# A fused attention and FFN kernel: v loaded by head over 128 partitions, and the order of loads and casts that goes with it

## The chip, the cores and the metric

The kernel runs on one core of one Trainium2 chip. The metric is the time of one execution in device microseconds. A core has five engines with an instruction queue each: TensorE (PE, its weight loads PEld), VectorE (DVE), ScalarE (ACT), GpSimd (POOL) and SyncE (SP), which here only issues DMAs. The DMAs themselves run on 16 DMA engines.

## The reference

Attention with a polynomial sketch as its feature map, over 4 batches, 4 heads, 1088 tokens and heads of 32, followed by a gated FFN on the 4352 tokens of width 128:

```
def phi(x):                                   # 64 features of a token
    a = einsum('rd,bhsd->bhsr', S1, x)        # r = 8
    b = einsum('rd,bhsd->bhsr', S2, x)
    return einsum('bhsi,bhsj->bhsij', a, b).reshape(..., 64)
q_p, k_p = phi(q), phi(k)
kv  = einsum('bhsf,bhsd->bhfd', k_p, v)
z   = sum(k_p, axis=2)
out = einsum('bhsf,bhfd->bhsd', q_p, kv) / (einsum('bhsf,bhf->bhs', q_p, z) + 1e-6)

x = out, tokens by 128 (4 heads x 32)
y = (maximum(x @ w_gate, 0) * (x @ w_val)) @ w_out      # d_ff = 1536, float32 in and out
```

## The kernel before

**Layout of the tokens.** A batch's 1088 tokens of a head lie over 32 partitions, 34 (NC) consecutive tokens each. For k and q the four heads are stacked, so partition 32 h + p holds tokens 34 p to 34 p + 33 of head h, and one load fills 128 partitions with rows of 4352 bytes. v is wanted the other way round: partition 32 a + p holds, for each of the four heads, tokens 34 p + 9 a to 34 p + 9 a + 8 (KX = 9 columns of 32 numbers, 1152 bytes). The tile `v32[b]` is therefore [128, 4 heads, 288]. The fourth block (a = 3) runs two tokens over the end of its row, and the last two columns of those partitions are left out later by `KV_ROWS`; for the very last row of v the two tokens don't exist, so that load is shorter and line 309 clears the place.

`load_v(eng, b, a)` (L212 to L218) loads one block a: 32 partitions, 4 heads, 288 numbers. Four of them load a batch, in the order 0, 2, 1, 3.

**Stages.** For each batch: class `K` takes k: DVE transposes in blocks of 32 (`t1`, L525), TensorE applies the sketch (`sk`, L536), DVE transposes back (`t2`, L549), `z` and `w` make the denominator's vector (L564, L578), POOL or DVE builds the 64 features (`phi`, L593), ACT casts v to float16 (`vc`, L599, two heads at a time), and TensorE sums features times v (`kv`, L606), which DVE writes into a block-diagonal tile `bz` (L613). Class `Q` does the same for q (L728, L734, then the denominator on POOL and DVE), and class `G` builds the q features for a group of up to 512 tokens (L859, POOL), has them transposed, multiplies them by `bz` (`num`, L893), and ACT writes the result to `xT` (L905), the input of the FFN. The transposes of the first three groups are done by TensorE (L877, copied out by ACT, L884), those of the other seven by a transposing DMA that SP issues (`xpose`, L867).

Class `F` is one FFN unit, 512 columns: `g` (L950, TensorE) and `relu` (L955, ACT), `v` (L962, TensorE), the product on DVE (L972) or, for every sixth unit, on POOL after a copy by ACT (L967, L977), and `o` (L984), which adds up w_out's part. There are 103 units. Units 0 to 23 belong to batch 0, 24 to 95 to batches 1 to 3, and the last 7 to the tokens left over from all batches. After a group's last unit ACT copies the sum (L992) and SP stores it with four DMAs of 32 partitions (L1001), the last group with one (L1006).

**The order of the work.** Nothing is ordered by hand on the five engines. Class `Plan` holds every operation with its engine, an assumed duration, its predecessors, its PSUM banks and a due time, runs through them in a simulated order of time, and the instructions are then issued in that order; each engine works its own list strictly in order. The assumed times are the small functions `dve`, `act`, `pool`, `pe16`, the constants T0, U and D1 (first unit, distance of units, a later shift), and the table LAND of landing times of the first loads. In the planned gaps of TensorE before the first unit, `warm` (L326 to L331) puts dummy matmuls.

The first loads are issued by SP in the order of the text: k of batch 0 in two parts, q of batch 0 in two parts, v of batch 0, w_gate and w_val thirds 0 and 1, w_out third 0, k of batch 1, the last thirds, and q of batch 1. The weights are float32 in DRAM; they are loaded into tiles of later batches (`wst`: k_sb and q_sb of batch 3, k_sb of batch 2, v32 of batches 1 and 2) and cast from there (`CAST`). A later load into such a tile waits for the cast. The later loads (`load`) are planned on SP with the stores and the transposing DMAs.

**DMAs and semaphores.** In the built program SP's transfers go round eight semaphores. Each transfer waits until the one that used its semaphore before, the eighth back, has landed.

Of the kernel before, what the change touches and what calls it, by code (L numbers as in the profile page):

```python
# [146 lines left out]
def kernel(  # L147
# [12 lines left out]
    nc = tc.nc  # L160

    B, H, S, D = q.shape
# [48 lines left out]

    def load_v(eng, b, a):  # L212
        w = KX * D
        n = w if a < 3 or b < B - 1 else (KX - 2) * D
        src = v[b, 0]
        eng.dma_start(
            out=v32[b][32 * a:32 * a + 32, :, 0:n],
            in_=bass.AP(src.tensor, src.offset + a * w, [[NC * D, 32], [S * D, H], [1, n]]))  # L218

# [55 lines left out]
    def load_vs(b):  # L275
        for a in (0, 2, 1, 3):
            load_v(nc.sync, b, a)

# [104 lines left out]
    l_sx = Lease()  # L383
    T0, U, SLACK = 11.0, 0.68, 0.25
    D1 = 0.2

# [11 lines left out]
    def act(cols):  # L398
        return cols / 1200.0 + 0.045

    def pool(cols):
        return cols * 0.00188 + 0.07

    LAND = {"k0a": 3.6, "S": 4.3, "k0b": 4.25, "q0a": 5.6, "q0b": 7.35, "v0": 9.95,
            "wg0": 10.35, "wv0": 11.0, "wg1": 11.65, "wv1": 12.3, "wo0": 12.95, "k1": 15.6,
            "wg2": 16.25, "wv2": 16.9, "wo1": 17.5, "wo2": 18.1, "q1": 19.5}
    land = {n: P.landed(n, t) for n, t in LAND.items()}
    P.free["DMA"] = LAND["q1"]

    def bank(l, i=0):  # L410
# [22 lines left out]


    def load(name, fn, after):
# [7 lines left out]
    load("v2", lambda: load_vs(2), [wcast["wg2"], wcast["wv2"], land["v1"]])  # L443
    load("k3", lambda: load_k(nc.sync, 3), [wcast["wg0"], wcast["wv0"], land["q2"]])
    load("q3", lambda: load_q(nc.sync, 3), [wcast["wg1"], wcast["wv1"], land["q2"]])
    load("v3", lambda: load_vs(3), [land["v2"]])

    class K:


        def __init__(self, b, prev):
# [179 lines left out]
    class Q:  # L631
# [3 lines left out]
        def __init__(self, b, x0, n, i, ks, qt1, old):  # L635
# [9 lines left out]
            if first:  # L645
                la, lc = Lease(), Lease()
                self.la, self.lc = la, lc
                s1 = [P.add("PE", f"qsk {name} {x}", 0.48, lambda x=x: self.sk_tok(x, x + 2),
                            qt1 + [wb_op], take=[la]) for x in range(0, n, 2)]
                t2 = P.add("ACT", f"qt2 {name}", act(2 * cols), self.t2_tok, s1 + old, drop=[la],  # L650
                           rec=0.13)
                la.left += n
                lt = Lease()
                self.lt = lt
                at = P.add("PE", f"qaT {name}", 0.85, self.aT, qt1 + [sa_op], take=[lt])
                ate = P.add("ACT", f"qaTe {name}", act(256), self.aTe, [at], drop=[lt], rec=0.13)
                s2 = [P.add("PE", f"qc {name}", 0.45, self.cx, [ate, ks[0].zc_op], take=[lc])]
                o1 = P.add("DVE", f"bw {name}", dve(cols) + 0.03, self.mul_ps, s2 + [t2] + old,
                           drop=[lc], rec=0.09)
                e, eng = "DVE", nc.vector  # L660

            else:
                self.l4 = [Lease(2), Lease(2)]
                s1 = P.add("PE", f"qsk {name}", cols / 600.0 + 0.28 + 0.37 * (n > NX),
                           self.sk, qt1 + wcs + [wq_op], take=self.l4)
# [133 lines left out]
    class G:  # L799


        def __init__(self, qs, b, ks, x0, n, i, col, old, how):
# [12 lines left out]
            else:  # L815
                phis.append(P.add("POOL", f"qphi {name}", pool(n * 256),
                                  lambda: self.phi(nc.gpsimd, 0, n), [qs.o4] + old))
            if how == "DMA":
                pt = P.add("SP", f"qtd {name}", 1.28, self.xpose, phis + old, rec=0.7)
                pt = P.add("DMA", f"qtd {name}", 0.6, None, [pt], rec=0.5)  # L820
            else:
# [85 lines left out]
    class F:  # L907


        def __init__(self, u, grp, qg, js, prev, old):  # L910
# [13 lines left out]
                      due=t + 0.35)  # L924
            vv = P.add("PE", f"v {u}", cost, self.v, [qg.x_op, wcast[f"wv{third}"]], take=[lv], due=t + 0.2)
            if self.pool:
                a2 = P.add("ACT", f"vcp {u}", act(cols), self.vcp, [vv], drop=[lv], rec=0.13,
                           due=t + 0.6)
                h = P.add("POOL", f"hp {u}", 1.18, self.hp, [a, a2, old], due=t + 1.3)
            else:  # L930
# [112 lines left out]
    for n, (b, x0, w, parts) in enumerate(sets):  # L1043
# [6 lines left out]
        for gb, y, m in parts:  # L1050
# [43 lines left out]
    for o in todo:  # L1094
        if o.eng == "PE":
            if not kept and o.start < f0 + 0.1:
                warm(int((o.start - at) * (1200 if o.start < WARM else 2280)))
# [33 lines left out]
```

## Time and profile before

| | |
|---|---|
| median of 3 runs (lowest, highest) | 102.06 us (101.67, 102.32) |
| profiled execution: time, span | 102.56 us, 100.8 us |
| granted TensorE clock | 1.00 throughout |
| busy: PE, PEld, DVE, ACT, POOL | 95.1, 66.4, 83.8, 82.2, 59.9 us |
| DMA | 13.28 MB, 16783 packets |
| HBM read, written | 9.14 MB, 2.23 MB |
| first FFN matmul (L950) | 13.76 us |
| v of batch 0: first issue, first cast | 2.63 us, 9.99 us |
| dummies (L330) | 85 matmuls, 7.7 us |

Times inside a profile count from the start of the span. Busy time of an engine is the time in which at least one of its instructions runs; PE's instructions overlap, so a busy PE is not PE at its peak. "Idle before" a group is idle time of its engine, put down to what ended it. A DMA's time to landing counts from its issue, so it holds its wait behind earlier transfers. SPq is SP's sequencer: what it shows is the time to issue a DMA, not the transfer.

### The profile page before, as it was taken

What the parts mean: (1) busy time and instruction counts of PE and PEld (TensorE: products, weight loads), DVE (VectorE), ACT (ScalarE), POOL (GpSimd) and SP (SyncE); (2) the same over time, 40 slices, a digit from 0 to 9 for tenths busy, and PEclk for the clock granted to TensorE, in tenths of its full rate; (3) what the DMA queues carried; (4) which work ended last, traced back from release to release, by engine and by line L of the source; (5) the groups of instructions that cost most, each with busy time, mean ns of one, the idle gap of its engine ahead of it and who ended that gap; (6) DMA issues with size and microseconds to landing.
All of it is one profiled execution on the core that took longest, in us unless ns stands there. A gap on an engine that the chain in (4) does not pass through costs nothing.

```text
span 100.8 us, 3139 instructions
## 1 busy us (share of the span) xinstructions
PE 95.1 (94%) x1191; PEld 66.4 (66%) x1191; DVE 83.8 (83%) x181; ACT 82.2 (82%) x162; POOL 59.9 (59%) x64
## 2 busy tenths in 40 slices
PE   6999997999999899999999999999999999999960
PEld 6959895678775466656756676667666666667940
DVE  5989959899999989999998679978768587795960
ACT  3411968997999978999977769899899999989940
POOL 7157269399999399349973993489960314033100
PEclk9999999999999999999999999999999999999999
DMA  2999999499943696300426003001481300120031
GB/s 44 321 272 294 408 403 417 166 309 272 386 131 108 145 136 163 104 7 0 104 52 156 7 0 104 7 7 37 121 182 37 81 24 0 52 59 0 4 100 52
DMA packets 16783, 13.28 MB, mean 132 GB/s; under 512 B 8064, under 2 KB 14464, under 8 KB 16768
## 3 DMA queue, kind: packets, MB, share of 16 engines
q1 hardware_dynamic: 16736, 13.08, 45.8%
q8 instruction: 9, 0.15, 0.6%
q14 instruction: 6, 0.05, 0.1%
q10 hardware_dynamic: 32, 0.00, 0.0%
HBM read 9.14 MB, written 2.23 MB: 113 GB/s over the span
## 4 chain that ended last, share of the span: by engine, by line
PE 78%; POOL 7%; ACT 5%; DMA 3%; issue 2%; DVE 2%; ACTq 0%
PE ps L984 19%; PE ps L950 18%; PE ps L962 17%; PE ps L330 7%; POOL qqp L859 4%; PE ps L893 3%; ACT g_sb L955 3%; PE ps L728 3%; DMA qpt<-qqp 3%; PE ps L536 2%; PE ps L606 2%; POOL kp L593 1%; PE ps L564 1%; PE ps L877 1%; DVE qabc L734 1%
## 5 line engine op out<-in xcount | busy, mean ns | idle before, releaser
L972 DVE TENSOR_TENSOR ht<-g_sb,ps 128x512 f16<-128x512 f16 (+1 forms) x87 | 55.4, 672 | 10.1 <-ACT g_sb L955 5.5
L955 ACT ACTIVATE g_sb<-ps 128x512 f16<-128x512 f32 (+1 forms) x103 | 57.1, 610 | 4.9 <-PE ps L950 4.1
L950 PE MATMUL ps<-xT,wg 128*128 128x512 f16 (+1 forms) x120 | 38.3, 348 | 0.4 <-ACT wg L425 0.4
L984 PEld LDWEIGHTS <-ht 128*128 128x128 f16 x408 | 28.8, 98 | 14.0 <-POOL ht L977 2.5
L984 PE MATMUL ps<-wo,ht 128*128 128x128 f16 x408 | 36.5, 219 | 0.2
L962 PE MATMUL ps<-xT,wv 128*128 128x512 f16 (+1 forms) x120 | 36.5, 348 | 0.0
L977 POOL TENSOR_TENSOR ht<-g_sb,v_sb 128x512 f16<-128x512 f16 x16 | 18.7, 1170 | 19.3 <-ACT v_sb L967 13.2
L593 POOL TENSOR_TENSOR kp<-kab 128x512 f16<-128x512 f32 (+1 forms) x15 | 17.1, 1162 | 5.0 <-DVE kab L549 5.0
L962 PEld LDWEIGHTS <-wv 128*128 128x128 f16 x120 | 13.0, 115 | 5.1 <-issue 1.1
L859 POOL TENSOR_TENSOR qqp<-qan,qabc 128x1024 f16<-128x1024 f32 (+1 forms) x9 | 15.7, 1763 | 0.1
L950 PEld LDWEIGHTS <-wg 128*128 128x128 f16 x120 | 13.1, 114 | 3.7 <-issue 0.9
L967 ACT COPY v_sb<-ps 128x512 f32<-128x512 f32 x16 | 9.7, 605 | 0.0
L330 PE MATMUL ps<-zero 128*128 128x128 f16 (+2 forms) x85 | 7.7, 257 | 1.0 <-DVE maskkv L295 1.0
L330 PEld LDWEIGHTS <-zero 128*128 128x128 f16 x85 | 6.7, 119 | 1.4 <-DVE maskkv L295 1.0
L992 ACT ACTIVATE o_sb<-ps 128x512 f32<-128x512 f32 (+1 forms) x10 | 5.5, 546 | 1.9 <-PE ps L984 1.9
L599 ACT CAST v<-v 128x576 f16<-128x576 f32 x8 | 5.3, 700 | 1.5 <-DMA v<-in_v_dram 1.4
L734 DVE STREAM_TRANSPOSE qabc<-ps 128x512 f32<-128x512 f32 (+2 forms) x8 | 5.4, 695 | 0.7 <-PE ps L728 0.6
L1024 DVE STREAM_TRANSPOSE qT<-q_sb 128x576 f32<-128x576 f32 (+4 forms) x10 | 6.0, 611 | 0.0
L905 ACT CAST xT<-ps 128x512 f16<-128x512 f32 (+1 forms) x9 | 4.9, 550 | 1.1 <-PE ps L893 1.1
L893 PE MATMUL ps<-qpt,bz 128*128 128x512 f16 (+2 forms) x26 | 5.3, 305 | 0.4 <-DMA qpt<-qqp 0.4
L525 DVE STREAM_TRANSPOSE kT<-k_sb 128x544 f32<-128x544 f32 (+2 forms) x8 | 5.6, 725 | 0.0
L606 PEld LDWEIGHTS <-kp 128*128 128x128 f16 (+1 forms) x72 | 3.6, 98 | 1.3 <-issue 0.2
(85 smaller groups left out, 63.9 us busy)
## 6 DMA issues: line engine op xcount, KB each, us to landing
v<-in_v_dram SPq DMA_DIRECT2D x15, 144.0 KB, 4.5
out_dram<-o_sb SPq DMA_DIRECT2D x28, 64.0 KB, 1.7
k_sb<-in_k_dram SPq DMA_DIRECT2D x3, 544.0 KB, 5.4
q_sb<-in_q_dram SPq DMA_DIRECT2D x3, 544.0 KB, 7.1
k_sb<-in_moe_w_out_dram SPq DMA_DIRECT2D x2, 256.0 KB, 5.9
q_sb<-in_q_dram SPq DMA_DIRECT2D x1, 416.0 KB, 5.2
k_sb<-in_k_dram SPq DMA_DIRECT2D x1, 288.0 KB, 2.9
k_sb<-in_k_dram SPq DMA_DIRECT2D x1, 256.0 KB, 3.0
```

The costliest lines, as they stand in the source:

```text
L330: nc.tensor.matmul(PS[:, W_BANK, 0:m], zero, zero[:, 0:m], start=True, stop=True)
L593: eng.tensor_tensor(out=self.kp[:, lo:hi].rearrange("p x g (i a c) -> p (x g i) a c", i=2, a=R), in0=src[:, 0, :, :, None].to_broadcast([1 ...
L734: nc.vector.transpose(self.abc[:, 0:self.n, 2 * i:2 * i + 2].rearrange("p x h f -> p h x f"), PS[:, b0:b1 + 1, 0:self.n * 32].rearrange("p ...
L859: eng.tensor_tensor(out=self.qp[:, lo:hi].rearrange("p x g (i a c) -> p (x g i) a c", i=2, a=R), in0=a_in[:, :, :, None].to_broadcast([128 ...
L893: nc.tensor.matmul(o[:, 0:n * 128].rearrange("f (x t) -> f x t", x=n)[:, :, t], self.ks[b or 0].bz[:, p], self.pt[:, 0:n, p, t], start=(p ...
L950: nc.tensor.matmul(bank(self.lg)[:, y * W:(y + 1) * W], wblock(wg, j), x, start=True, stop=True, skip_group_check=True)
L955: nc.scalar.activation(out=self.gs[:, 0:self.cols], in_=bank(self.lg)[:, 0:self.cols], func=ACTF.Relu)
L962: nc.tensor.matmul(bank(self.lv)[:, y * W:(y + 1) * W], wblock(wv, j), x, start=True, stop=True, skip_group_check=True)
L967: nc.scalar.copy(out=self.vs, in_=bank(self.lv))
L972: nc.vector.tensor_tensor(out=self.ht[:, 0:w], in0=self.gs[:, 0:w], in1=bank(self.lv)[:, 0:w], op=ALU.mult)
L977: nc.gpsimd.tensor_tensor(out=self.ht, in0=self.gs, in1=self.vs, op=ALU.mult)
L984: nc.tensor.matmul(o[:, s], self.ht[:, y * W + s * 128:y * W + (s + 1) * 128], wo[:, j // 4, (j % 4) * DM:(j % 4 + 1) * DM], start=(j == 0 ...
```

## The change

- `load_v` takes a head instead of a block: one DMA for all 128 partitions of one head, 1152 bytes each, into the same tile in the same layout. The DRAM side of it is written as 4 blocks (step 288) by 32 rows (step 1088) by 288 numbers. The last head of the last batch is split into 96 and 32 partitions, so there are 17 v loads instead of 16.
- The plan lets the cast of the first pair of heads of batch 0 depend on the first two loads alone (`v0a`, `v0b`).
- The weights' last thirds of w_gate and w_val and the second third of w_out are issued ahead of k of batch 1.
- `warm` makes dummies of up to 512 columns, by reading the zero tile repeatedly, and leaves 0.1 us of each later gap free.
- The casts of wv0 and wv1 move from POOL to ACT, that of wv2 from ACT to POOL; of the two blocks of batch 0's k features that DVE made, one goes to POOL.
- The loads of k, q and v of batch 3 are planned after the transposing DMA of the group `gs[4]` (the second of batch 1).
- Assumed times in the plan: the table LAND, U, D1, `act`, a v load's issue (0.62 instead of 0.44 each) and transfer, and some others.

```
-    def load_v(eng, b, a):
+    def load_v(eng, b, h):
         w = KX * D
-        n = w if a < 3 or b < B - 1 else (KX - 2) * D
-        src = v[b, 0]
-        eng.dma_start(
-            out=v32[b][32 * a:32 * a + 32, :, 0:n],
-            in_=bass.AP(src.tensor, src.offset + a * w, [[NC * D, 32], [S * D, H], [1, n]]))
+        src = v[b, h]
+
+        for lo, hi, n in [(0, 4, w)] if (b, h) != (B - 1, H - 1) else [(0, 3, w), (3, 4, w - 2 * D)]:
+            eng.dma_start(
+                out=v32[b][32 * lo:32 * hi, h, 0:n],
+                in_=bass.AP(src.tensor, src.offset + lo * w, [[w, hi - lo], [NC * D, 32], [1, n]]))
...
-    for a in (0, 2, 1, 3):
-        load_v(nc.sync, 0, a)
+    for h in range(H):
+        load_v(nc.sync, 0, h)
...
     load_w(0)
     load_w(1)
     load_wo(0)
-    load_k(nc.sync, 1)
     load_w(2)
     load_wo(1)
+    load_k(nc.sync, 1)
     load_wo(2)
...
     def load_vs(b):
-        for a in (0, 2, 1, 3):
-            load_v(nc.sync, b, a)
+        for h in range(H):
+            load_v(nc.sync, b, h)
...
-    nc.vector.memset(v32[B - 1][96:128, :, (KX - 2) * D:], 0.0)
+    nc.vector.memset(v32[B - 1][96:128, H - 1, (KX - 2) * D:], 0.0)
...
         while n >= 32:
-            m = min(n // 32 * 32, 128)
-            nc.tensor.matmul(PS[:, W_BANK, 0:m], zero, zero[:, 0:m], start=True, stop=True)
-            n -= m
+            m, w = (min(n // 128, 4), 128) if n >= 128 else (1, n // 32 * 32)
+            nc.tensor.matmul(PS[:, W_BANK, 0:m * w], zero,
+                             zero[:, None, 0:w].to_broadcast([128, m, w]), start=True, stop=True)
+            n -= m * w
...
-    T0, U, SLACK = 11.0, 0.68, 0.25
-    D1 = 0.2
+    T0, U, SLACK = 11.0, 0.69, 0.25
+    D1 = 0.7
...
-    CAST = {"wg0": "ACT", "wv0": "POOL", "wg1": "ACT", "wv1": "POOL", "wo0": "POOL",
-            "wg2": "ACT", "wv2": "ACT", "wo1": "ACT", "wo2": "POOL"}
+    CAST = {"wg0": "ACT", "wv0": "ACT", "wg1": "ACT", "wv1": "ACT", "wo0": "POOL",
+            "wg2": "ACT", "wv2": "POOL", "wo1": "ACT", "wo2": "POOL"}
...
-        i = P.add("SP", f"{name} issue", 0.44 * n, fn, after, rec=1.95 - 0.44 * n)
-        land[name] = P.add("DMA", name, 2.7 if n == 4 else 1.4, None, [i], rec=0.15)
+        issue[name] = i = P.add("SP", f"{name} issue", (0.62 if n == 4 else 0.44) * n, fn, after,
+                                rec=(1.95 - 0.62 * n if n == 4 else 1.5))
+        land[name] = P.add("DMA", name, 1.5 if n == 4 else 1.4, None, [i], rec=0.15)
...
-            own = [3, 4] if b == 0 else []
+            own = [4] if b == 0 else []
...
-            vc = [P.add("ACT", f"vc {b} {h}", 0.58, lambda h=h: self.vc(h), [land[f"v{b}"]],
-                        rec=0.13) for h in range(2)]
+            vc = [P.add("ACT", f"vc {b} {h}", 0.58, lambda h=h: self.vc(h),
+                        [land[f"v{b}" if b else f"v0{'ab'[h]}"]], rec=0.13) for h in range(2)]
...
+    for n in ("k3", "q3", "v3"):
+        issue[n].after.append(gs[4].turn)
+        gs[4].turn.succ.append(issue[n])
```

SP's order after the first loads, in the built programs: before, q of batch 2, k2, v1, k3, q3, four stores, v2, four stores, two transposing DMAs, v3; after, q2, k2, v1, v2, eight stores, two transposing DMAs, k3, q3, v3.

More of the change, by code (lines that the diff above doesn't have):

```diff
@@ L398, in act @@
     def act(cols):
-        return cols / 1200.0 + 0.045
+        return cols / 1200.0 + 0.062
     def pool(cols):
         return cols * 0.00188 + 0.07
-    LAND = {"k0a": 3.6, "S": 4.3, "k0b": 4.25, "q0a": 5.6, "q0b": 7.35, "v0": 9.95,
-            "wg0": 10.35, "wv0": 11.0, "wg1": 11.65, "wv1": 12.3, "wo0": 12.95, "k1": 15.6,
-            "wg2": 16.25, "wv2": 16.9, "wo1": 17.5, "wo2": 18.1, "q1": 19.5}
+    LAND = {"k0a": 3.6, "S": 4.3, "k0b": 4.25, "q0a": 5.2, "q0b": 6.9, "v0a": 7.7, "v0b": 8.45,
+            "wg0": 9.3, "wv0": 9.94, "wg1": 10.58, "wv1": 11.22, "wo0": 11.86, "wg2": 12.5,
+            "wv2": 13.14, "wo1": 13.78, "k1": 16.14, "wo2": 16.78, "q1": 18.14}
     land = {n: P.landed(n, t) for n, t in LAND.items()}
@@ L443 @@
     load("v2", lambda: load_vs(2), [wcast["wg2"], wcast["wv2"], land["v1"]])
-    load("k3", lambda: load_k(nc.sync, 3), [wcast["wg0"], wcast["wv0"], land["q2"]])
-    load("q3", lambda: load_q(nc.sync, 3), [wcast["wg1"], wcast["wv1"], land["q2"]])
+    load("k3", lambda: load_k(nc.sync, 3), [wcast["wg0"], wcast["wv0"]])
+    load("q3", lambda: load_q(nc.sync, 3), [wcast["wg1"], wcast["wv1"]])
     load("v3", lambda: load_vs(3), [land["v2"]])
@@ L815, in __init__ @@
             else:
-                phis.append(P.add("POOL", f"qphi {name}", pool(n * 256),
+                phis.append(P.add("POOL", f"qphi {name}", pool(n * 256) - 0.02 * n,
                                   lambda: self.phi(nc.gpsimd, 0, n), [qs.o4] + old))
@@ L819, in __init__ @@
                 pt = P.add("SP", f"qtd {name}", 1.28, self.xpose, phis + old, rec=0.7)
+                self.turn = pt
                 pt = P.add("DMA", f"qtd {name}", 0.6, None, [pt], rec=0.5)
@@ L924, in __init__ @@
                       due=t + 0.35)
-            vv = P.add("PE", f"v {u}", cost, self.v, [qg.x_op, wcast[f"wv{third}"]], take=[lv], due=t + 0.2)
+            vv = P.add("PE", f"v {u}", cost, self.v, [qg.x_op, wcast[f"wv{third}"]], take=[lv], rec=0.07,
+                       due=t + 0.2)
             if self.pool:
@@ L928, in __init__ @@
                            due=t + 0.6)
-                h = P.add("POOL", f"hp {u}", 1.18, self.hp, [a, a2, old], due=t + 1.3)
+                h = P.add("POOL", f"hp {u}", 1.13, self.hp, [a, a2, old], rec=0.06,
+                          due=t + 1.3)
             else:
```

6 lines of the change are left out of this document (4 added, 2 removed).

## The prediction

> **What bounds the kernel now.** I read the page first, then the chain of waits in order of time, the DMA views, and SP's and ACT's timelines around the place where the chain leaves TensorE.
>
> ```profile
> span 100.8 us, 3139 instructions
> PE 95.1 (94%) x1191; PEld 66.4 (66%) x1191; DVE 83.8 (83%) x181; ACT 82.2 (82%) x162; POOL 59.9 (59%) x64
> ```
>
> TensorE is busy almost throughout, so anything that only shifts work elsewhere is worth nothing unless it moves the times at which TensorE gets its inputs. The chain shows where those decide:
>
> ```profile
> 26.50 0.59 POOL qan L794
> 27.09 0.06 POOL ht L977
> 27.15 1.02 issue
> 28.17 3.88 POOL qqp L859 x2
> 32.05 0.28 POOL ht L977
> 32.33 2.79 DMA qpt<-qqp
> 35.12 0.04 issue
> 35.17 0.60 PE ps L893 x2
> ```
>
> Line 893 at 35.17 makes the features of batch 1, the first of the last 79 FFN units. From there the chain is TensorE almost without a break to 97.4, so the time is "arrival of batch 1" plus a tail of about 62 us. A later arrival moves the end one for one once units 0 to 23 have run out. Here TensorE had run out only just:
>
> ```profile
> 14.00:18.00 4.00, 3.07 (x32) 2.40 (x29) 3.18 (x6) 3.39 (x7) 3.79 (x5) 1.00 1.04 408
> ...
> 32.00:35.20 3.20, 2.80 (x36) 1.35 (x34) 3.20 (x6) 3.20 (x8) 1.52 (x3) 1.00 0.54 124
> ```
>
> (The first figure after the length is TensorE's busy time, the last two are DMA share and GB/s.) It idled 0.9 us in one stretch and 0.4 us in the other; so little slack can hide nothing large.
>
> The arrival hangs on SP's queue. Its first transposing DMA is issued at 32.33, though the first qqp was done at about 30.1 (half of 3.88 after 28.17):
>
> ```profile
> 25.61 4.66 SPq L216 DMA_DIRECT2D v<-in_v_dram  x4
> 30.37 1.79 SPq L1001 DMA_DIRECT2D out_dram<-o_sb  x4
> 32.33 2.68 SPq L867 DMA_TRANSPOSE qpt<-qqp  x2
> ```
>
> SP hands its transfers to eight semaphores in turn, and each waits for the one eight back to land. So batch 2's fourth v load waited for q of batch 3 ("SPq L216 <- DMA q_sb<-in_q_dram: 1.9" in SP's waits), the stores stood behind it, and the transposes behind them.
>
> **The change, part by part.**
>
> *The v loads.* Before, one load is 32 partitions by 4 heads by 1152 B. After, it is one head: 128 partitions by 1152 B, but the DRAM side counts 4 column blocks, then 32 rows. Outermost counts were 32 on both sides; now they are 4 and 128. What decides is over how many of the 16 DMA engines such a load is dealt.
>
> ```profile
> q1 hardware_dynamic: 16736, 13.08, 45.8%
> q8 instruction: 9, 0.15, 0.6%
> q14 instruction: 6, 0.05, 0.1%
> q10 hardware_dynamic: 32, 0.00, 0.0%
> ...
> s<-in_S_dram ACTq DMA_DIRECT2D x2, 1.0 KB
> ```
>
> q10 carried the two S loads, each 8 rows of 128 B: 16 packets of data. The other 16 are completions, 8 per load, so a load with an outer count of 8 ran on 8 engines. No row has unequal counts. The two ends are 16 engines (as for the 128-row loads) and 4 (as many as the DRAM side has outer steps). I take 4: the row says that the outer count is what is dealt, and a side with four steps cannot be dealt to more than four engines.
>
> The Trainium skill ("DMA: Bandwidth & Descriptors", section "Why a DMA increments its semaphore by 16 and not by 1") states it as a rule: the engine count is the largest number up to 16 that divides the slowest count above 1 of both sides. By it this load gets 4 engines, always the same lowest ones (and batch 3's last load of 96 rows gets 3); q10's 8 agrees, and no run here shows unequal sides.
>
> Price of one head: 147.5 KB over 4 engines is 36.9 KB each. An engine's rate comes from two stretches:
>
> ```profile
> 5.00:10.00 5.00, 4.97 (x98) 3.79 (x105) 4.62 (x18) 0.66 (x3) 3.45 (x4) 1.00 1.06 280
> 10.00:14.00 4.00, 4.00 (x96) 3.66 (x97) 3.56 (x13) 3.34 (x7) 1.21 (x2) 1.00 1.04 405
> ```
>
> All 16 are full in both (share over 1). 405/16 = 25.3 GB/s with weights, 280/16 = 17.5 with v. That gives 1.46 or 2.11 us a head. I take 1.75: the slow stretch has 16 engines writing into the same 32 partitions, while four engines write to four groups of 32, but the rows stay short. Four heads are 7.0 us, against 2.6 now (v lands from 7.3 to 9.9).
>
> In the trace the big loads land in the order of their issue, and a load that uses all engines ends with its last one, so everything issued later waits on these four. In steps:
> 1. k of batch 0 has landed by 4.2; its q (557 KB at 405 GB/s, 1.4 us) is through at 5.6 to 7.3, say 6.0. v of batch 0: second head 9.5, fourth 13.0 (before: 9.9).
> 2. Eight weight loads at 0.65 (262 KB at 405): 18.2. This is where the reorder puts k of batch 1: 19.6 (15.3 before), wo2 20.2, q of batch 1 21.6 (19.1 before), q and k of batch 2 23.0 and 24.4. Their issues are free in time: k waits for casts that end by about 21, v1 for the cast of wo2, by about 22, each some 2 us from issue to data.
> 3. v of batches 1 and 2: eight heads, 14.0 us: 38.4.
> 4. After the change SP's order is v1, v2, eight stores, transposes, then k3, q3, v3. The eighth store waits for the transfer eight back: batch 2's fourth v head. So the first transpose cannot be issued before 38.4 + 0.45 (one store's issue), and lands 2.8 later: 41.65 against 35.12. **+6.5 us.**
> 5. In ACT's order 22 relus stand ahead of batch 1's xT (L905), 23 before. One unit more is left for the tail: three groups of 0.22 on TensorE, **+0.7**.
>
> Nothing covers this: units 0 to 23 stand behind ACT, whose v casts wait too (batch 1's at 27.9 and 31.4, batch 2's at 34.9 and 38.4). Behind each wait the relus, hence DVE's products and TensorE.
>
> *Other edits, with one answer.* The casts of wv0 and wv1 move from POOL to ACT (0.6 each) and wv2 to POOL; one 128x512 kphi goes from DVE (0.69) to POOL (1.07); the dummies fall from 85 matmuls to 20 of up to 512 columns (7,648 columns instead of 10,624); T0, U, D1 and the durations only change the planned order. All but one lie in the first 24 units, which now end before batch 1 arrives, so I put 0 on them; with that cover gone they are worth -0.5 to +1 (two casts of 0.6 ahead of the first relu against POOL freed). SP's issue of a v load is 0.43 here; the new form isn't in the trace, 0.33 to 0.6 (the S loads' largest), and hidden by 1.75 a head. v of batch 3 follows k3 and q3, issued after the transposes: its heads land at some 48 to 53, its casts stand near 50 and 58, so 0 (up to +1). A wait may also cost clock: the first 28 dummies take 113 ns each (3.17 us), the last 22 take 54. A slow first stretch after 41.7 would add up to 1.7; TensorE waits about 2 us there, so I take 0.
>
> The Trainium skill ("TensorE: Matmul & The Clock Gate", Part 1) halves the clock after about 3.4 us of idling; by that a wait of 2 us costs nothing and one twice as long the 1.7. The PEclk row here never falls below 9, so no run shows it.
>
> **Sum.** 6.5 + 0.7 = 7.2 on the profiled execution's 102.56 (span 100.8 and 1.8 around it) gives 109.8. That execution lies 0.5 above the median of 102.06, so **109.3 us**.
>
> **Rivals.**
> - *Sixteen engines, and the change does what it says* (the other side). A head is 0.36 us, v of batch 0 takes 1.5 instead of 2.6, the weights land about 1.1 earlier, and the transposes go out when qqp is done: 2.2 earlier than 32.33. TensorE can take 1.2 from an earlier start and 1.3 from its idle time, so about -2.2: **99.9**. For it: 128 partitions on the SBUF side, and loads over 128 partitions reach 405 GB/s. It decides as soon as a v load uses eight or more engines. Against: q10.
> - *Four engines at the weights' rate.* 1.46 a head: v0 at 11.8, v2 at 23.2 + 11.7 = 34.9, arrival 38.2: +3.1 + 0.7, **105.9**. For: the writes no longer meet in 32 partitions.
> - *Four engines at the rate of v now.* 2.11 a head: v0 at 14.4, v2 at 25.8 + 16.9 = 42.7, arrival 45.9: +10.8 + 0.7, up to 1.7 more for the clock: **113.6 to 115**. For: 280 GB/s is the only rate the trace has with 1152 B rows.
>
> **How the numbers follow.** Four engines have 0.90: the middle case 0.62, the fast one 0.13, the slow one 0.15. Sixteen have 0.08; 0.02 is left for about no change. A change of 1%, about 1 us, is what a measurement of this kernel can tell. Faster 0.08, same 0.03, slower 0.89. The likeliest four-engine case reaches from 106 to 113; the range takes in the fast one and most of the slow one: 105 to 114.5, leaving the 16 engines outside.
>
> **What would show it.** Right: four completions instead of 16 per v load (fewer packets on q1: of 256 completions of v loads 79 are left, 15 loads with 4, one with 3, one with 16); the DMA share near 0.25 with under 110 GB/s while v1 and v2 move; issue to landing of v well over 4.5; ACT's v casts waiting for the DMA; SP's stores waiting for v; line 893 for batch 1 near 41.7; a tail of 62 us as before. Wrong: v landing before 10 us and transposes issued near 30. If v does land late but batch 1 arrives near 35, then the wait behind the eighth store is misread.

## The result, and the profile after

The changed kernel took 113.83 us (median of 3 runs, 113.09 to 114.08) against 102.06 before (101.67 to 102.32): a ratio of 1.1142, 95% interval 1.1043 to 1.1241. It is slower by 11.8 us; 109.3 was forecast, with a range of 105 to 114.5. Here and below medians and ranges hold all runs of a kernel, while a ratio leaves slow runs out and can stand below that of the medians.

The page of the changed kernel (its profiled execution took 113.83, as the median) begins so. The PEclk row of section 2 is the granted clock in 40 slices:

```profile
span 112.0 us, 3027 instructions
PE 97.3 (87%) x1126; PEld 63.9 (57%) x1126; DVE 83.4 (74%) x180; ACT 83.5 (75%) x163; POOL 60.4 (54%) x64
...
PEclk9999556999999995899999999999999999999997
...
q1 hardware_dynamic: 16559, 13.10, 39.2%
```

TensorE is no longer full (87%, was 94%), it ran twice at half clock, and q1 carries 16736 - 16559 = 177 packets fewer for the same work.

The chain of waits over the stretch that was shown of before, and SP's timeline beside it (start, length, line, transfer, how many):

```profile
34.02 0.63 POOL qan L799
...
34.72 1.96 POOL qqp L865
36.68 1.13 POOL ht L985
37.81 1.80 POOL qqp L865
39.61 2.83 DMA qpt<-qqp
42.44 0.05 issue
42.49 1.03 PE ps L899 x2
```

```profile
23.43 8.22 SPq L217 DMA_DIRECT2D v<-in_v_dram  x8
31.75 7.69 SPq L1009 DMA_DIRECT2D out_dram<-o_sb  x8
39.61 2.69 SPq L873 DMA_TRANSPOSE qpt<-qqp  x2
```

Batch 1's features come at 42.49 instead of 35.17. The first qqp was done at 36.68, its transposing DMA went out at 39.61, behind the eight stores: SP held it for 2.9, where it had held it for 2.2 before (30.1 to 32.33). But qan itself is 7.5 later than before (34.02 for 26.50), so SP's queue is not the first cause. That lies at the start. ACT's timeline there and TensorE's first FFN matmul, before (the bracket is the idle time ahead, and what ended it):

```profile
8.36 0.27 ACT L719 COPY qabc<-ps 128x128 f32<-128x128 f32 x1 [1.15 <-PE ps L712]
9.99 1.25 ACT L599 CAST v<-v 128x576 f16<-128x576 f32 x2 [1.37 <-DMA v<-in_v_dram]
...
13.76 0.39 PE L950 MATMUL ps<-xT,wg 128*128 128x256 f16 x2
```

and after:

```profile
6.52 0.38 ACT L748 ACTIVATE aT<-ps 128x256 f32<-128x256 f32 x1 [1.62 <-PE ps L744]
10.48 0.67 ACT L604 CAST v<-v 128x576 f16<-128x576 f32 x1 [3.58 <-DMA v<-in_v_dram]
11.06 0.26 ACT L724 COPY qabc<-ps 128x128 f32<-128x128 f32 x1
14.62 0.67 ACT L604 CAST v<-v 128x576 f16<-128x576 f32 x1 [3.30 <-DMA v<-in_v_dram]
15.20 0.61 ACT L427 CAST wg<-k_sb 128x512 f16<-128x512 f32 x1
...
19.23 0.38 PE L958 MATMUL ps<-xT,wg 128*128 128x256 f16 x2
```

After the change ACT stands idle twice for a v cast, with qabc's copy and the first weight casts behind it; before, the copy ran ahead of the casts. The first unit starts at 19.23 instead of 13.76.

Stretches of the changed kernel, with TensorE's busy time first after the length, and at the end granted clock, DMA share and GB/s:

```profile
10.00:14.00 4.00, 2.78 (x50) 1.83 (x50) 1.52 (x7) 0.84 (x2) 0.23 (x1) 0.72 1.02 287
14.00:18.00 4.00, 2.66 (x20) 2.15 (x20) 1.55 (x5) 3.38 (x8) 0.45 (x1) 0.50 0.83 292
...
23.00:40.00 17.00, 15.67 (x223) 10.38 (x220) 15.05 (x28) 14.92 (x30) 13.63 (x12) 1.00 0.37 121
...
43.00:46.00 3.00, 3.00 (x15) 1.51 (x13) 1.31 (x2) 1.68 (x3) 1.28 (x2) 0.52 0.83 267
```

The span can be split by TensorE's records: the start of the first FFN matmul, its busy time from there to its last matmul, the sum of its gaps in the same stretch, and what is left. Before: 13.76 + 82.37 + 1.56 + 3.09 = 100.78. After: 19.23 + 83.56 + 5.58 + 3.68 = 112.05. So of the 11.3 us, 5.5 are lost ahead of the first unit, 4.0 in waits behind it, 1.2 in longer busy time (the half clock at 42.5 is in it), 0.6 at the end. This split is used for all runs below.

### The profile page after: what moved, and what is told of

Same layout as the page of the kernel before. It is cut to its first block, busy times and chain, and to the rows that moved or that the text cites. A ratio compares the mean times of both kernels' runs of the same rounds, so it can differ in the third digit from the quotient of the medians.

```text
span 112.0 us, 3027 instructions
## 1 busy us (share of the span) xinstructions
PE 97.3 (87%) x1126; PEld 63.9 (57%) x1126; DVE 83.4 (74%) x180; ACT 83.5 (75%) x163; POOL 60.4 (54%) x64
## 3 DMA queue, kind: packets, MB, share of 16 engines
q1 hardware_dynamic: 16559, 13.10, 39.2%
## 4 chain that ended last, share of the span: by engine, by line
PE 58%; DMA 14%; POOL 11%; issue 4%; ACT 4%; SPq 3%; DVE 2%; POOLq 0%; ACTq 0%
PE ps L992 15%; PE ps L958 15%; PE ps L970 15%; DMA v<-in_v_dram 9%; POOL qqp L865 6%; DMA qpt<-qqp 5%; PE ps L899 4%; POOL ht L985 3%; ACT g_sb L963 3%; PE ps L733 2%; SPq L217 2%; PE ps L331 1%; PE ps L541 1%; DVE ht L980 1%; POOL qan L799 1%
## 5 line engine op out<-in xcount | busy, mean ns | idle before, releaser
L958 PE MATMUL ps<-xT,wg 128*128 128x512 f16 (+1 forms) x120 | 39.5, 352 | 1.2 <-ACT v_sb L975 1.2
L970 PE MATMUL ps<-xT,wv 128*128 128x512 f16 (+1 forms) x120 | 39.3, 351 | 0.0
L992 PEld LDWEIGHTS <-ht 128*128 128x128 f16 x408 | 29.4, 99 | 17.1 <-DVE ht L980 3.0
L992 PE MATMUL ps<-wo,ht 128*128 128x128 f16 x408 | 37.7, 221 | 0.4 <-DVE ht L980 0.2
L598 POOL TENSOR_TENSOR kp<-kab 128x512 f16<-128x512 f32 (+1 forms) x16 | 18.0, 1153 | 4.8 <-DVE kab L554 2.5
L899 PE MATMUL ps<-qpt,bz 128*128 128x512 f16 (+2 forms) x26 | 6.0, 334 | 4.0 <-DMA qpt<-qqp 4.0
L611 PE MATMUL ps<-v,kp 128*128 128x64 f16 (+1 forms) x72 | 5.2, 202 | 4.5 <-ACT v L604 4.5
L611 PEld LDWEIGHTS <-kp 128*128 128x128 f16 (+1 forms) x72 | 4.3, 104 | 6.6 <-issue 5.3
L331 PE MATMUL ps<-zero 128*128 128x512 f16 (+6 forms) x20 | 6.7, 469 | 1.0 <-DVE maskkv L296 1.0
```

Of the source, the lines that this page charges most:

```text
L331: nc.tensor.matmul(PS[:, W_BANK, 0:m * w], zero, zero[:, None, 0:w].to_broadcast([128, m, w]), start=True, stop=True)
L598: eng.tensor_tensor(out=self.kp[:, lo:hi].rearrange("p x g (i a c) -> p (x g i) a c", i=2, a=R), in0=src[:, 0, :, :, None].to_broadcast([1 ...
L611: nc.tensor.matmul(m[:, 64 * p:64 * p + 64], self.kp[rows, x, p], v16[self.b][rows, 2 * p:2 * p + 2, x * D:(x + 1) * D], start=(x == 0 and ...
L899: nc.tensor.matmul(o[:, 0:n * 128].rearrange("f (x t) -> f x t", x=n)[:, :, t], self.ks[b or 0].bz[:, p], self.pt[:, 0:n, p, t], start=(p ...
L958: nc.tensor.matmul(bank(self.lg)[:, y * W:(y + 1) * W], wblock(wg, j), x, start=True, stop=True, skip_group_check=True)
L970: nc.tensor.matmul(bank(self.lv)[:, y * W:(y + 1) * W], wblock(wv, j), x, start=True, stop=True, skip_group_check=True)
```

## Experiments

**Where the v loads and SP's queue stand (e1, e3, e4, e5).** The first theory was the prediction's: four engines make v late, SP's queue passes it on to batch 1, and that is the loss.

e1 is the changed kernel with the old loads, 32 partitions by four heads (edit in part):

```diff
-    def load_v(eng, b, h):
+    def load_v(eng, b, a):
...
-    for h in range(H):
-        load_v(nc.sync, 0, h)
+    for a in (0, 2, 1, 3):
+        load_v(nc.sync, 0, a)
```

> The changed kernel with the v loads of the kernel before (32 partitions by four heads each) and everything else of the change kept: SP's order, the casts, the weights ahead of batch 1's keys, the dummies. My theory (the v loads run on four DMA engines, and that alone is the loss): v of batch 0 lands near 10, the first transposing DMA goes out when the first qqp is done, near 30, line 899 for batch 1 starts at 32.5 to 33.5, nothing waits ahead of batch 3, and the time is 99.5 to 101. Rival (the new order of SP's loads or of the casts costs by itself): line 899 for batch 1 at 36 or later and 104 or more. Either way all 256 completions of v loads are back on q1.

Measured: 107.98 us (107.11 to 109.10), ratio 1.0547 (1.0457 to 1.0637). All 16736 packets are back on q1, so the four completions come from the new form of the load, but the theory fell: with 16 engines the rest of the change still costs 5.5%. ACT in e1:

```profile
9.94 0.67 ACT L603 CAST v<-v 128x576 f16<-128x576 f32 x1 [2.99 <-DMA v<-in_v_dram]
10.52 0.26 ACT L723 COPY qabc<-ps 128x128 f32<-128x128 f32 x1
10.68 0.67 ACT L603 CAST v<-v 128x576 f16<-128x576 f32 x1
```

v lands when it did before (9.9), but the cast stands ahead of qabc's copy in ACT's order; before, the copy ran at 8.36, while ACT was waiting. The first unit starts at 16.50, 2.7 late, with v on time. TensorE waited 2.55 meanwhile, and 3.41 at half clock came behind that wait.

e3 is the kernel before with only the move of batch 3's loads (edit in part):

```diff
+    for n in ("k3", "q3", "v3"):
+        issue[n].after.append(gs[4].turn)
+        gs[4].turn.succ.append(issue[n])
```

> The kernel before with one part of the change: k, q and v of batch 3 are planned behind the transposing DMAs of the first group of batch 1; v loads, casts, weights and dummies as before. My theory (batch 1's arrival hangs on SP's queue, and the 2.2 us between the first qqp and its transposing DMA are given back): first transposing DMA near 30 instead of 32.33, line 893 for batch 1 near 33, time 99.5 to 101. Rival (TensorE has no slack there anyway, or batch 3's later loads cost at the end what is gained): 101.5 to 103.

Measured: 102.53 us (101.94 to 103.48), ratio 1.0042 (1.0003 to 1.0081). The transposing DMA went out at 31.38 instead of 32.33 and line 896 started at 34.46, 0.7 earlier than before; nothing came of it. TensorE's gaps behind the first unit are 1.69 (before 1.56): the earlier arrival took no waiting time away. The rival was right.

e4 is the changed kernel with `"v2"` added to that list of loads behind the transposing DMAs.

> The changed kernel with the four v loads of batch 2 moved behind the transposing DMAs of batch 1, ahead of k, q and v of batch 3. My theory (the stores and the transposing DMAs behind them wait, through SP's eight semaphores, for batch 2's v): the first transposing DMA goes out when the first qqp is done, near 36.7 instead of 39.61; line 899 for batch 1 at about 39.5 instead of 42.49; batch 2's v, issued from about 39, lands near 46 to 47, ahead of its need; time about 110.5 to 111.5 against 113.8. First rival (SP waits for work of its own, not for v2): line 899 stays within 1 of 42.5 and the time within 1 of 113.8. Second rival (batch 2 comes too late and gives it back): line 899 early, a new wait of TensorE for batch 2, time 113 or more.

Measured: 113.59 us (112.53 to 114.68), ratio 1.1023 (1.0951 to 1.1094). SP's, TensorE's and ACT's lines:

```profile
37.76 3.17 SPq L873 DMA_TRANSPOSE qpt<-qqp  x2
...
40.65 0.61 PE L899 MATMUL ps<-qpt,bz 128*128 128x512 f16 x2 [0.43 <-DMA qpt<-qqp]
...
51.29 0.67 ACT L604 CAST v<-v 128x576 f16<-128x576 f32 x1 [1.98 <-DMA v<-in_v_dram]
...
52.99 0.38 PE L970 MATMUL ps<-xT,wv 128*128 128x512 f16 x1 [1.91 <-ACT xT L911]
```

The stores did wait for batch 2's v: without it the transposing DMAs go out 1.85 earlier and batch 1 comes 1.84 earlier. But the late v then holds a cast for 1.98, and TensorE 1.91 at 52.99. So the waits are given back, as the second rival said: the gaps behind the first unit are 5.42, against 5.58. The time isn't quite: the four runs took 112.53, 112.57, 114.61 and 114.68, so the lower two are 1.3 below the changed kernel's median. In the profiled one (112.53) TensorE's busy time is 0.85 lower, with the half clock at 42.5 gone, and the end 0.5 shorter. The theory's range holds none of the four runs, the rival's two.

e5 is the changed kernel with dummies in the wait for batch 1 (NWARM is 9):

```diff
+            if self.col == 1024:
+                for _ in range(NWARM):
+                    nc.tensor.matmul(o, zero, zero[:, None].to_broadcast([128, 4, 128]),
+                                     start=True, stop=True, skip_group_check=True)
```

> The changed kernel with nine dummy matmuls of 512 columns ahead of batch 1's first matmul of line 899, to fill the 2.2 us in which TensorE waits for it; they write a bank that line 899 then writes anew. My theory (the idle time of 2.2 us costs 3.4 us of half clock, 1.7 us of work): granted clock 1.0 between 42.5 and 46, time 1.2 to 2 below the changed kernel, about 112. Rival (the half clock there is a throttle that busy dummies bring too, or the work behind hides it): clock still near 0.5 in that stretch, or clock 1.0 and the time within 0.5 of 113.8.

Measured: 111.81 us (110.72 to 113.75), ratio 1.0951 (1.0846 to 1.1056). The median is 2.0 below the changed kernel, but the runs spread (110.72, 111.13, 112.50, 113.75) and the two intervals overlap at the edge. The same three microseconds as in the last row of the stretches above:

```profile
43.00:46.00 3.00, 3.00 (x40) 1.80 (x40) 1.91 (x4) 2.12 (x4) 1.25 (x2) 1.00 0.90 223
```

Forty matmuls instead of 15 in the same time, at clock 1.00. The half clock there was the effect of the wait, and it cost time: without the dummies TensorE's busy time behind the first unit is 81.99, 1.6 less than the changed kernel's 83.56. That is near the 1.7 of the expectation.

**What the plan believed (e6, e7, e2, e12).** The changed kernel's order comes from a table of landing times. It has v of batch 0 at 7.7 and 8.45; on the chip the two pairs were cast from 10.48 and 14.62 on, each as it landed, and with the old loads both landed by 9.9. New theory: a cast that is planned too early stands at the head of ACT's queue and holds what could have run.

e6 is e1 with the landing times of e1's own trace (edit in part; the later weights, k and q of batch 1 and the assumed time of a v issue, 0.44 for 0.62, go with them):

```diff
-    LAND = {... "v0a": 7.7, "v0b": 8.45, "wg0": 9.3, ...}
+    LAND = {... "v0a": 9.85, "v0b": 9.85, "wg0": 10.35, ...}
...
-        land[name] = P.add("DMA", name, 1.5 if n == 4 else 1.4, None, [i], rec=0.15)
+        land[name] = P.add("DMA", name, 2.7 if n == 4 else 1.4, None, [i], rec=0.15)
```

> The changed kernel with the v loads of the kernel before (as in e1), and with landing times in the plan as e1's trace shows them (v of batch 0 at 9.85 for both pairs instead of 7.7 and 8.45; k of batch 1 at 16.8; later v loads 2.7 instead of 1.5). ACT's planned order then has qabc's copy ahead of both v casts, as in the kernel before. Theory A (e1's loss is the order that the plan makes of landing times which do not come true: ACT stands 3.0 at a v cast with qabc's copy behind it): TensorE's first FFN unit starts near 14 as before, instead of 16.5 in e1, ACT's idle time ahead of the first v cast falls under 1.5, time 101.5 to 104. Rival (the weights ahead of batch 1's keys, or the casts of wv on ACT, cost it): first unit at 16 or later, or batch 1 still late, time 106 or more.

Measured: 104.24 us (103.63 to 105.56), ratio 1.0188 (1.0137 to 1.0240), just above the range given. ACT in e6, and the first unit:

```profile
8.11 0.27 ACT L723 COPY qabc<-ps 128x128 f32<-128x128 f32 x1 [0.62 <-PE ps L716]
10.06 1.24 ACT L603 CAST v<-v 128x576 f16<-128x576 f32 x2 [1.68 <-DMA v<-in_v_dram]
...
13.39 0.38 PE L957 MATMUL ps<-xT,wg 128*128 128x256 f16 x2
```

The first unit starts at 13.39, 3.1 earlier than in e1 with the same loads at the same times. Theory A holds: the plan's landing times are worth 3.7 us, with not one transfer of another shape. The half clock of e1 is in that figure, since with the wait it went too. Neither the weights ahead of batch 1's keys nor wv's casts on ACT delay the start.

e7 is the changed kernel with landing times of its own trace (edit in part):

```diff
-    LAND = {... "v0a": 7.7, "v0b": 8.45, "wg0": 9.3, ...}
+    LAND = {... "v0a": 10.4, "v0b": 14.55, "wg0": 15.0, ...}
...
-        land[name] = P.add("DMA", name, 1.5 if n == 4 else 1.4, None, [i], rec=0.15)
+        land[name] = P.add("DMA", name, 6.6 if n == 4 else 1.4, None, [i], rec=0.15)
```

> The changed kernel with its v loads by head, and with landing times in the plan as its own trace shows them (v of batch 0 at 10.4 and 14.55, weights from 15.0 on, k of batch 1 at 20.7, a later v 6.6 instead of 1.5). Theory A (about half of the loss is the planned order, half the four engines): qabc's copy is done near 9 instead of 11.3, the first unit starts at 17 to 17.7 instead of 19.2, TensorE's waits behind it are 3 in sum instead of 5.6, time 107.5 to 110. Rival (the four engines set all of it, since the first unit needs the second pair of heads, which lands at 14.55 either way): first unit within 0.7 of 19.2 and time 112 or more.

Measured: 107.73 us (107.51 to 107.83), ratio 1.0547 (1.0508 to 1.0587): 6.1 below the changed kernel, with the same transfers over the same four engines. ACT and the first unit:

```profile
8.29 0.27 ACT L724 COPY qabc<-ps 128x128 f32<-128x128 f32 x1 [0.51 <-PE ps L717]
...
14.31 0.67 ACT L604 CAST v<-v 128x576 f16<-128x576 f32 x1 [2.39 <-DMA v<-in_v_dram]
...
17.12 0.38 PE L958 MATMUL ps<-xT,wg 128*128 128x256 f16 x2
```

The copy is back ahead of the casts, the gaps behind the first unit are 2.65 and the granted clock is 1.00, so the 6.1 hold the order and the half clocks that its waits had brought. Against e6, which differs in the loads (and the table that fits them), the four engines cost 107.73 - 104.24 = 3.5.

e2 is the kernel before with only the loads by head (the first hunk of the change):

> The kernel before with its v loads by head and nothing else of the change: the plan, SP's order, casts and dummies as before. Theory A: v of batch 0 lands at 14.6, not 9.9, the first unit starts at 17.5 to 18.5 (before 13.8, after 19.2), the q1 completions fall by 177, and with the waits for v1 and v2 behind it the time is 107.5 to 111, below the changed kernel. Rival (the old order is worse for late loads, since k of batch 1 goes ahead of weights and k and q of batch 3 ahead of v2): 113 or more.

Measured: 114.46 us (113.56 to 114.87), ratio 1.1197 (1.1143 to 1.1251). Theory A missed and the rival's range was right: the loads alone, under a plan that does not know of them, cost as much as the whole change. First unit at 19.07; two of TensorE's waits are

```profile
15.05 0.63 PE L607 MATMUL ps<-v,kp 128*128 128x64 f16 x9 [3.18 <-ACT v L600]
...
45.54 0.80 PE L894 MATMUL ps<-qpt,bz 128*128 128x512 f16 x2 [4.03 <-DMA qpt<-qqp]
```

and half clock went with each. Part of the rival's reason shows in the second: the first qqp of batch 1 was done at 34.89, but its transposing DMA went out at 40.16, behind batch 2's v, which in the old order is issued after k and q of batch 3. The first unit is 1.95 later than e7's, with the second pair cast at the same time (14.32 and 14.31). In e7 ACT's copy of rdx ran at 10.08, ahead of both casts, in e2 at 14.90, behind them: the planned order again, and the half clock that the wait brought. No run sets these two apart.

e12 is the kernel before with one number changed:

```diff
-  "v0": 9.95
+  "v0": 7.7
```

> The kernel before with one number changed: the plan's landing time of v of batch 0 is 7.7 (as the change has it for the first pair) instead of 9.95. Loads, SP's order and all else as before; the plan now puts both v casts ahead of qabc's copy in ACT's order. Theory A (what a planned landing that does not come true costs, alone): the casts still start near 10, qabc's copy moves from 8.4 to about 11.2, the first unit starts at 15.8 to 16.8 instead of 13.8, the time is 104 to 106. Rival (the first unit waits for v in any case, so nothing is lost): first unit within 0.5 of 13.8, time within 1 of the kernel before.

Measured: 107.08 us (106.65 to 108.14), ratio 1.0466 (1.0397 to 1.0535). ACT:

```profile
6.66 0.38 ACT L743 ACTIVATE aT<-ps 128x256 f32<-128x256 f32 x1 [1.77 <-PE ps L739]
10.72 1.25 ACT L599 CAST v<-v 128x576 f16<-128x576 f32 x2 [3.68 <-DMA v<-in_v_dram]
11.87 0.26 ACT L719 COPY qabc<-ps 128x128 f32<-128x128 f32 x1
```

One planned landing, 2.25 too early, costs 4.4 us (the kernel before took 102.65 in the same rounds), and no transfer was changed. It is more than expected, and the first unit comes at 19.84, not at 16: TensorE waited 3.23 for this cast and then ran 6.8 us at half clock, which the expectation had not counted. In the profiled execution, the slowest of the four, v itself landed at 10.66, 0.7 later than before, so that much of its delay isn't the order. Behind the first unit the gaps are 0.99, so the whole loss is at the start.

**The clock and the second wait (e11, e10).**

e11 is the changed kernel with its own dummy routine called in the two waits for v:

```diff
+            if self.b == 0 and lo == 0:
+                warm(7168 if pp[0] == 0 else 4096)
```

> The changed kernel with 14 dummy matmuls of 512 columns ahead of the first matmul on batch 0's v (line 611) and eight ahead of the first on the second pair of heads, in the bank that the other dummies write; all else kept. They fill TensorE's waits of 3.1 and 1.4 for the v casts. Theory (part of the late start is the clock: after these waits TensorE runs 6.8 us at half clock, with the rest of batch 0's chain and the dummies behind it at double length): granted clock 1.0 from 8 to 20, first unit at 17.3 to 18.4 instead of 19.2, time 112.2 to 113. Rival (v's second pair and ACT's queue set the first unit, the clock only fills waiting time): first unit within 0.4 of 19.2, time within 0.6 of 113.8. Either way the time stays 4 or more above e7 (107.7), where the plan's landing times are as measured.

Measured: 111.64 us (109.54 to 112.25, 7 runs), ratio 1.0744 (1.0659 to 1.0829). The times fall in two groups, which the granted clock tells apart: five runs at 0.980 to 0.984 took 111.44 to 112.25, two at 0.993 and 1.000 took 109.54 and 110.20, which give the ratio. The profiled run is one of the five; its start, where line 331 is the dummies, and batch 1's wait:

```profile
8.10 3.25 PE L331 MATMUL ps<-zero 128*128 128x128 f16 x15
...
13.28 1.89 PE L331 MATMUL ps<-zero 128*128 128x512 f16 x8
...
18.41 0.38 PE L960 MATMUL ps<-xT,wg 128*128 128x256 f16 x2
```

The clock is 1.00 throughout the start and the first unit 0.8 earlier, at the late edge of the theory's 17.3 to 18.4. Its one half clock left comes at 42.0, with the wait of 2.16 for batch 1. So the early half clock is worth 0.8 us by the first unit and about 2 by the times (111.4 to 112.3 against 113.83), and with the late one gone too it is up to 4 in all. No trace was kept of the two runs without it, so a shorter wait may be in the 4. The expectation that at least 4 above e7 would stay was too high: 109.9, the mean of the two, is 2.1 above 107.73. The rest fits the order of the work, but e11 differs from e7 in the added dummies too.

e10 is the changed kernel with four stores moved behind the first transposing DMA of batch 3:

```diff
+    st5 = next(o for o in P.ops if o.name == f"st {sum(len(js) for js in units[:6]) - 1}")
+    st5.after.append(gs[7].turn)
+    gs[7].turn.succ.append(st5)
```

> The changed kernel with the last four stores ahead of batch 3's transposing DMAs moved behind the first of them, all else kept. Theory (the wait of 1.8 ahead of line 899 at 85 is SP's queue: stores that wait for their own output, and one issue of 2.0 beside an instruction fetch, stand ahead of transposing DMAs whose qqp was done 3.1 earlier): first transposing DMA of batch 3 issued within 1 of its qqp, no wait over 0.5 ahead of batch 3's line 899, 1 to 1.8 less than the changed kernel, about 112 to 112.8. Rival (POOL's qqp or something else sets it, or the time is lost further on): wait still over 1, or the time within 0.7 of 113.8.

Measured: 111.99 us (111.82 to 112.74), ratio 1.0944 (1.0884 to 1.1004), 1.8 below the changed kernel. Batch 3's wait in the changed kernel, and the same place in e10, SP and TensorE:

```profile
85.06 0.61 PE L899 MATMUL ps<-qpt,bz 128*128 128x512 f16 x2 [1.79 <-DMA qpt<-qqp]
```

```profile
79.98 2.05 SPq L873 DMA_TRANSPOSE qpt<-qqp  x1
82.14 2.27 SPq L1009 DMA_DIRECT2D out_dram<-o_sb  x4
...
83.52 0.59 PE L899 MATMUL ps<-qpt,bz 128*128 128x512 f16 x2
```

The transposing DMA goes out as its qqp is done (79.96) and the wait is gone. The wait was SP's queue.

**Is there a version that wins (e8, e9)?**

e8 is the kernel before with v of batch 0 as eight loads of two heads and 32 partitions:

```diff
-    for a in (0, 2, 1, 3):
-        load_v(nc.sync, 0, a)
+    for h in (0, 2):
+        for a in (0, 2, 1, 3):
+            load_v(nc.sync, 0, a, h, 2)
```

> The kernel before with v of batch 0 loaded by pair of heads and 32 partitions (eight loads of two heads, 16 engines each, in place of four loads of four heads), the plan told that the first pair lands at 8.6 and the second at 9.95. It does what the change set out to do without the four engines. Theory A: the first cast starts at 8.7 to 9.2, the second near 10, the first unit at 13.2 to 13.7 instead of 13.8, time 101.3 to 102. Rival (four more issues of SP and the weights behind them cost as much, or xT's other inputs set the first unit): first unit at 13.8 or later, time 102 to 103.

Measured: 109.02 us (106.42 to 110.12, 6 runs), ratio 1.0632 (1.0566 to 1.0698). Both theories missed. SP in the profiled run (106.42, the fastest of the six):

```profile
2.63 4.80 SPq L216 DMA_DIRECT2D v<-in_v_dram  x8
7.48 0.43 SPq L257 DMA_DIRECT2D k_sb<-in_moe_w_gate_dram  x1
7.95 1.43 SPq L258 DMA_DIRECT2D k_sb<-in_moe_w_val_dram  x1
```

The eighth load needs the semaphore of the transfer eight back, the second part of q, which landed at 7.10; it was issued at 7.12. The first weights went out at 7.48 instead of 4.53, and the DMA share from 5 to 10 us is 0.72 where before it is 1.06. The first pair of heads was cast at 8.19, but the first unit came at 14.97. This version loses more than an earlier half of v brings. How much of that is the semaphores' is not shown: its plan still has the weights at their old times (the second third of w_gate at 11.65; it landed at 12.34, and ACT stood 0.52 at its cast). A table that fits was not run.

e9 is e6 with later v loads planned to land after 4.2 instead of 2.7 and with e10's move of four stores.

> e6 (the change with the 16-engine loads and landing times as measured) with two more edits: a later v load counts 4.2 in the plan instead of 2.7, which puts batch 1's casts six FFN relus later in ACT's order, and the last four stores ahead of batch 3's transposing DMAs go behind the first of them. Expected: e6's TensorE waits of 0.8 at 25.8 and 0.9 at 75.4 both go, the idle time behind the first unit falls from 3.2 to about 1.5 as in the kernel before, time 101.5 to 102.8, no different from the kernel before or a little better. Rival (the casts, now later, make batch 1 or 2 late): a new wait near 31 to 36 and 103.5 or more.

Measured: 102.79 us (102.02 to 103.78), ratio 1.0015 (0.9977 to 1.0054): as the kernel before. The gaps fell from e6's 3.19 to 1.83, the first unit stands at 13.65. So all else in the change, with the old loads, a plan that fits the chip and the moved stores, is worth nothing either way, and no version run here is faster than the kernel before.

| kernel | v loads | planned landing of v0 | us | first unit | gaps behind it | clock |
|---|---|---|---|---|---|---|
| before | 16 engines | 9.95 | 102.06 | 13.76 | 1.56 | 1.000 |
| e9 | 16 | 9.85 | 102.79 | 13.65 | 1.83 | 1.000 |
| e6 | 16 | 9.85 | 104.24 | 13.39 | 3.19 | 0.991 |
| e12 | 16 | 7.7 | 107.08 | 19.84 | 0.99 | 0.968 |
| e1 | 16 | 7.7 / 8.45 | 107.98 | 16.50 | 3.67 | 0.978 |
| e7 | 4 | 10.4 / 14.55 | 107.73 | 17.12 | 2.65 | 1.000 |
| after | 4 | 7.7 / 8.45 | 113.83 | 19.23 | 5.58 | 0.948 |
| e2 | 4 | 9.95 | 114.46 | 19.07 | 6.73 | 0.970 |

(Times are medians; first unit, gaps and granted clock are those of the profiled execution. In the rounds of the experiments the kernel before took 102.1 to 102.7.) Down the table the 11.8 us split into 2.2 from the kernel before to e6, most of which e9 gets back with two more edits, 3.5 from e6 to e7 for the four engines, and 6.1 from e7 to the changed kernel for landing times that did not come true.

## Why the prediction was right, and where it was not

*Sign and mechanism of the loads: right.* Four engines per v load: q1 lost exactly the 177 completions named; e2, which has only these loads, shows the same 16559, and e1 has all 16736 back. The DMA share was named as near 0.25 with under 110 GB/s; from 23 to 40 it was 0.37 and 121, with stores and k of batch 2 in the same stretch. The rule of the Trainium skill ("DMA: Bandwidth & Descriptors", "Why a DMA increments its semaphore by 16 and not by 1") is borne out here for sides with unequal counts.

*Step 1, the price of a head: too low.* The two pairs of batch 0 were cast at 10.48 and 14.62: 2.07 a head, near the upper bound (2.11), not 1.75. Second head 10.4 for 9.5, fourth 14.5 for 13.0. *Step 3* made up for it: later heads took 1.6 (stores issued at 35.88, 37.44 and 39.13, each when a head had landed), and batch 2's v was through at 39.1 for 38.4. At the start all 16 engines were full (share 1.02 from 10 to 14), later they were not (0.37): other loads on the same engines would explain the two prices, but no run tested it.

*Step 4, the eighth store: right in place, wrong in weight.* First transposing DMA at 39.61 for 38.85, batch 1 at 42.49 for 41.65. But e4 takes this wait away and batch 1 comes only 1.84 earlier. The first qqp itself was done 6.5 later than before (36.68 for 30.1), behind a first unit that is 5.5 late, and no order of SP's could have sent it sooner. The prediction followed the transfers alone, found that they end at 38.4, and did not ask when the qqp would be done.

*The failed step: "other edits, with one answer", put at 0.* It reasoned that casts and planned order lie in units that end before batch 1 arrives. They are not covered: batch 1's features stand behind those units on ACT, DVE and POOL. The one edit that mattered, the table of landing times, was not in the sum at all. It costs 3.7 us with 16 engines (e1 against e6) and 6.1 with four (after against e7); v of batch 0 alone, planned too early in the kernel before, costs 4.4 (e12). The four engines cost 3.5 under a plan that fits them (e7 against e6).

*The clock, put at 0 with a bound of 1.7: 1.6 for the late stretch by TensorE's busy time (e5), up to 4 with the early one (e11).* It is part of the 6.1, not on top of it. The sentence on the Trainium skill's clock gate ("TensorE: Matmul & The Clock Gate", Part 1) said that a wait of 2 us costs nothing by it; here a wait of 2.2 halved the clock for 3.41, and the measurement decides.

*The tail, put at 0.7 more for one unit: 3.9 longer.* From line 899 to the span's end it is 112.0 - 42.5 = 69.5, before 100.8 - 35.2 = 65.6. In it are the late half clock and batch 3's wait of 1.79, which was not foreseen (e10).

*The sixteen-engine rival, 99.9, is refuted:* the changed kernel on 16 engines is e1, 107.98. And its gain of 2.2 was not there to be had (e3). The rival at v's rate, 113.6 to 115, names the total best, by a price per head that held only for batch 0; its arrival of 45.9 did not come. So the total lay in the range in part by luck: the loads were dearer at the start, SP's wait was worth 1.8 of the 6.5 put on it, plan and clock were missing, and the tail was too short.

## What to carry to other kernels

Where an engine's order is written out from planned times, a planned landing is an edit like any other: compare each with the trace, and ask what stands behind the first instruction that will wait. Split the span by the busiest engine (start of its steady work, busy, gaps, end) before following a chain: the chain showed the last releaser at 39.61, the split showed that half of the loss was over by 19. And count a load's engines from its completions before spreading it over more partitions.

## What the hardware showed that was not expected

- **Waits and clock.** Over the 14 kernels, TensorE had 11 waits of 2.16 to 4.03 us behind its first work, and half clock followed or overlapped each; the five of 1.53 to 2.01 brought none. Half clock lasted 3.41, 6.83 or 10.24 us, one, two or three times 3.41, and which of them varied for like waits (2.55: 3.41; 2.61: 10.24).
- **Instruction fetches and SP.** The issue of the store at 78.95 in the changed kernel took 1.96 instead of 0.43, and beside it a 16 KB fetch on q8 ran from 78.89 for 1.66. In the kernel before, long issues at 10.94, 26.61 and 35.05 stand beside fetches at 10.79, 26.60 and 34.68. At the end of the changed kernel the store at 106.91 took 2.28 beside a fetch at 107.05, and the last store, whose output was ready at 108.78, went out at 109.30: that is most of the 0.6 lost at the end. That the one holds the other wasn't tested.
- **Issues while four engines are behind.** The last four of the eight v issues, from 25.76 on, took 1.2 to 1.7 each, where the second to fourth took 0.53. The first of these four has a fetch beside it (25.78), the others have none. In e1, with 16 engines, the same eight issues took 0.33 to 0.43 each but for the last (1.19, with a fetch at 23.69), so the long ones come with the loads by head. This looks like a full queue holding the issuer, which no run here tests.
